# Turning the result column of a decode block: one TensorE transpose and a copy in place of four VectorE transposes

## The chip, the cores and the metric

The kernel runs on one core of a Trainium2 chip. The metric is the device time of one execution in microseconds (us), on the device. The profile's span, from the first to the last instruction, is about 2 us shorter.

## The reference, cut to what matters

One token goes through a pre-norm attention block with a key/value cache of 65,536 positions and then through a gated feed-forward block. What matters here is the last line: the result is 1024 bfloat16 numbers, 2 KB.

```python
h  = x + attention(layernorm(x), k_cache, v_cache, wq, wo)      # 4 kv heads, Sk = 65536, Dh = 128
h2 = h + (gelu(hn @ w_gate) * (hn @ w_up)) @ w_down             # hn = layernorm(h); D = 1024, F = 3584
return h2                                                       # (1, 1, 1024), bfloat16
```

## The kernel before

The last product, with w_down, ends in column form. `dl_ps` is a tile of 128 partitions by 8 columns in PSUM: partition p of column c holds output number 128c + p. In memory, 128 consecutive numbers belong to one c. So the column has to be turned into 8 rows of 128 before the output DMA can write runs of 256 bytes. The kernel before does that with VectorE, in four transposes of 32x32 blocks:

```python
    o_blk = rows.tile([P, 32], BF16, name="o_blk")
    nc.vector.memset(o_blk[:], 0.0)
    o_tr = rows.tile([32, P], BF16, name="o_tr")
    # ... the matmuls of w_down: chunks 0..13 into d_ps, turned early into hd_cp with the residual;
    # ... chunks 14..27 into dl_ps, 8 matmuls of 128x1 for each chunk
    nc.vector.tensor_tensor(out=o_blk[:, 0:DC], in0=dl_ps[:], in1=hd_cp[:], op=ALU.add)
    for i in range(4):
        nc.vector.transpose(out=o_tr[:, 32 * i:32 * i + 32], in_=o_blk[32 * i:32 * i + 32, :])
    nc.sync.dma_start(out=out[0, 0].rearrange("(c p) -> c p", p=P), in_=o_tr[0:DC, :])
```

One more place matters, because it already does what the change will do. After the attention, `oT_all` (128x32, bfloat16) is turned by a TensorE transpose and copied out of PSUM:

```python
    nc.tensor.transpose(out=o_ps[:], in_=oT_all[:], identity=ident_bf[:])     # PSUM tile "oh_ps", 32x128 bf16
    nc.vector.tensor_copy(out=o_sb[:], in_=o_ps[:])
```

Of the kernel before, what the change touches and what calls it, by code (L numbers as in the profile page):

```python
# [9 lines left out]
ALU = mybir.AluOpType  # L10
AX = mybir.AxisListType
BF16 = mybir.dt.bfloat16
# [5 lines left out]
def kernel(  # L18
# [13 lines left out]
    nc = tc.nc  # L32
    P = 128
# [6 lines left out]
    DC = D // P  # L40
# [29 lines left out]
    ident_bf = lead.tile([P, P], BF16, name="ident_bf")  # L70
# [114 lines left out]
    for hf in range(2):  # L185
        for t in range(2):
            o = W2 * hf + rep * t
            nc.vector.tensor_copy(out=qsel[64 * t:64 * t + 64, :, :, hf, o:o + rep],
                                  in_=qsel_ps[64 * t:64 * t + 64, :, :].rearrange("p a (g h) -> p g a h", h=rep))
# [152 lines left out]
    rows = ctx.enter_context(tc.tile_pool(name="rows", bufs=1))  # L342
    ps_w = ctx.enter_context(tc.tile_pool(name="ps_w", bufs=4, space=PSUM))
    ps_t = ctx.enter_context(tc.tile_pool(name="ps_t", bufs=3, space=PSUM))
# [16 lines left out]
    for wc in range(Hq // WN):  # L361
        wv = load(wo_v[:, wc * WN:(wc + 1) * WN, :], "wo_sb")
        for cc in range(WN):
            c = wc * WN + cc
# [14 lines left out]
    def cp_sum(row, add, name):  # L379
        ps = ps_t.tile([P, 4, DS], F32, name=name + "_ps", tag="T")  # L380
        for b in range(4):
            nc.tensor.matmul(ps[:, b, :], lhsT=row[:, b * P:(b + 1) * P], rhs=hsel[:], start=True, stop=True)
        t = rows.tile([P, DC], F32, name=name)
        nc.vector.tensor_tensor(out=t[:].rearrange("p (s b) -> p b s", b=4), in0=ps[:],
                                in1=add[:].rearrange("p (s b) -> p b s", b=4), op=ALU.add)
        return t
# [56 lines left out]
    d_ps = row_bank("d_ps")  # L443
    dl_ps = ps_w.tile([P, DC], F32, name="dl_ps", tag="w")
    nc.vector.memset(dl_ps[:], 0.0)
    o_blk = rows.tile([P, 32], BF16, name="o_blk")
    nc.vector.memset(o_blk[:], 0.0)
    o_tr = rows.tile([32, P], BF16, name="o_tr")
    c0 = 0
    for sz in sizes:  # L450
        wv = load(wd_v[:, c0:c0 + sz, :], "wd_sb")
        for cc in range(sz):
            c = c0 + cc
# [7 lines left out]
        if c0 == NW:  # L461
            d_r = rows.tile([P, 512], F32, name="d_r")
            nc.vector.tensor_copy(out=d_r[:], in_=d_ps[:])
            hd_cp = cp_sum(d_r, h_cp, "hd_cp")
    nc.vector.tensor_tensor(out=o_blk[:, 0:DC], in0=dl_ps[:], in1=hd_cp[:], op=ALU.add)
    for i in range(4):
        nc.vector.transpose(out=o_tr[:, 32 * i:32 * i + 32], in_=o_blk[32 * i:32 * i + 32, :])
    nc.sync.dma_start(out=out[0, 0].rearrange("(c p) -> c p", p=P), in_=o_tr[0:DC, :])


# [28 lines left out]
```

## Time and profile before

| what | value | where read |
|---|---|---|
| time | 412.35 us, three runs from 412.31 to 412.57 | the runs |
| span of the profile | 410.6 us | the page |
| HBM traffic | 173.02 MB, 421 GB/s | the page |
| last TensorE burst ends, last add starts | 407.43, 407.47 us | timeline |
| end of the add to the issue of the output DMA | 0.94 us | timeline |
| issue to end of span | 2.0 us | timeline, span |

These are lines from the page of the kernel before. (PE is TensorE, PEld its weight load, DVE VectorE, ACT ScalarE, SP SyncE; a q at the end means that engine's instruction queue, from which DMAs are issued.) The first line is the busy share of the DMA engines in 40 equal slices of the span, in tenths; then the traffic; then the chain of work that ended last, by engine.

```profile
DMA  8999999999999999999999999999999999999993
...
HBM read 173.02 MB, written 0.00 MB: 421 GB/s over the span
...
DMA 51%; PE 21%; ACT 5%; DVE 4%; issue 1%; DVEq 0%
```

Memory is busy until the last slice, which alone shows 3 instead of 9. That last slice is 10 us long, and it is where the changed lines run. The timeline of the kernel before, for its last microseconds, has start, duration, engine, line, operation, output<-inputs and shapes, and in brackets how long the engine was idle and what released it:

```profile
406.42 1.01 PE L458 MATMUL dl_ps<-act_bf,wd_sb 128*128 128x1 bf16 x24 [0.18 <-DMA wd_sb<-in_B_w_down_dram]
407.47 0.17 DVE L465 TENSOR_TENSOR o_blk<-dl_ps,hd_cp 128x8 bf16<-128x8 f32 x1 [3.37 <-PE dl_ps L458]
407.67 0.84 DVE L467 STREAM_TRANSPOSE o_tr<-o_blk 32x32 bf16<-32x32 bf16 x4
408.58 0.36 SPq L468 DMA_DIRECT2D out_dram<-o_tr  x1
```

The reader is to see a strict sequence: matmuls, add, four transposes, DMA issue. No other engine works any more. The add ends at 407.47 + 0.17 = 407.64; 408.58 - 407.64 = 0.94 us is what the change can alter. The same timeline 65 us earlier shows the turn of `oT_all`, a ready-made price tag for the new sequence:

```profile
342.76 0.17 DVE L307 TENSOR_TENSOR oT_all<-o_ps,rl 128x8 bf16<-128x8 f32 x1 [1.97 <-PE o_ps L305]
...
342.98 0.29 PE L333 MATMUL oh_ps<-ident_bf,oT_all 128*32 128x128 bf16 x1 [0.26 <-DVE oT_all L307]
...
343.31 0.21 DVE L335 COPY o_sb<-oh_ps 32x128 bf16<-32x128 bf16 x1 [0.38 <-PE oh_ps L333]
```

From the end of that add (342.93) to the end of the copy (343.52) it is 0.59 us.

### The profile page before, as it was taken

To read this page: it belongs to the slowest core of one execution; us is meant where nothing else is said; L and a number is where in the kernel's file an instruction comes from. 1 tells how busy PE (TensorE), PEld (TensorE's weight loads), DVE (VectorE), ACT (ScalarE), POOL (GpSimd) and SP (SyncE) were. 2 spreads that over 40 slices of the span, in tenths; PEclk is the share of its full clock that TensorE was granted. 3 is DMA by queue.
4 is the path that set the end of the run, shared out by engine and by line. 5 is a ranking of instruction groups with operands and counts; after the bars stand their busy time and mean duration, and the time that the engine had idled before them with its cause. 6 is when DMAs were issued, how large, how long until landed. Compare 5 with 4: busy or idle time off the path is not lost.

```text
span 410.6 us, 6002 instructions
## 1 busy us (share of the span) xinstructions
PE 272.3 (66%) x2576; PEld 193.8 (47%) x2576; DVE 169.5 (41%) x296; ACT 163.0 (40%) x249; POOL 5.1 (1%) x16
## 2 busy tenths in 40 slices
PE   0448888797993938965868399394945536467365
PEld 0227666484673727645565277182822113163134
DVE  0213787766772636751627187344630001021011
ACT  0014676597570748642524775152738000000000
POOL 1000000000000000000000000000020000000000
PEclk9986999969998887996969689979875655556665
DMA  8999999999999999999999999999999999999993
GB/s 358 409 456 410 450 414 442 425 436 429 434 433 434 433 429 437 421 444 426 437 427 433 431 431 436 429 425 439 428 437 428 441 426 434 428 433 439 421 422 149
DMA packets 6682, 173.40 MB, mean 422 GB/s; under 512 B 896, under 2 KB 896, under 8 KB 1152
## 3 DMA queue, kind: packets, MB, share of 16 engines
q1 hardware_dynamic: 6496, 173.02, 98.0%
q8 instruction: 20, 0.33, 0.3%
q14 instruction: 6, 0.05, 0.0%
q10 hardware_dynamic: 160, 0.00, 0.0%
HBM read 173.02 MB, written 0.00 MB: 421 GB/s over the span
## 4 chain that ended last, share of the span: by engine, by line
DMA 51%; PE 21%; ACT 5%; DVE 4%; issue 1%; DVEq 0%
DMA k_sb<-in_A_k_cache_dram 27%; PE kt_ps L216 13%; DMA wu_sb<-in_B_w_up_dram 10%; DMA v_sb<-in_A_v_cache_dram 10%; DMA wd_sb<-in_B_w_down_dram 5%; ACT pT L272 4%; PE qk_ps L239 3%; PE acc_ps L289 2%; ACT kt_sb L220 2%; DVE mx L246 1%; PE wu_ps L158 1%; DVE kt_sb L222 1%; DVE sc_sb L245 1%; PE o_ps L305 1%; PE bc_ps L262 0%
## 5 line engine op out<-in xcount | busy, mean ns | idle before, releaser
L216 PE MATMUL kt_ps<-ident_f,k_sb 128*128 128x128 f32 x1024 | 144.7, 304 | 37.2 <-DMA k_sb<-in_A_k_cache_dram 34.2
L216 PEld LDWEIGHTS kt_ps<-ident_f,k_sb 128*128 128x128 f32 x1024 | 131.7, 159 | 57.8 <-issue 36.5
L220 ACT COPY kt_sb<-kt_ps 128x1024 bf16<-128x1024 bf16 x116 | 111.9, 1015 | 105.4 <-issue 74.7
L222 DVE COPY kt_sb<-kt_ps 128x1024 bf16<-128x1024 bf16 x140 | 95.3, 688 | 92.8 <-PE kt_ps L216 89.8
L272 ACT ACTIVATE pT<-sc_sb,nbias 128x256 bf16<-128x256 f32 x64 | 47.6, 745 | 23.7 <-DVE nbias L264 23.7
L239 PE MATMUL qk_ps<-kt_sb,qsel 128*32 128x512 bf16 x512 | 39.7, 384 | 9.9 <-ACT kt_sb L220 9.2
L289 PE MATMUL acc_ps<-v_sb,pT 128*32 128x512 bf16 x512 | 37.4, 441 | 12.1 <-DMA v_sb<-in_A_v_cache_dram 12.1
L246 DVE TENSOR_REDUCE mx<-sc_sb 128x8 f32<-128x512 f32 x32 | 35.2, 1099 | 0.5
L245 DVE STREAM_TRANSPOSE sc_sb<-qk_ps 128x512 f32<-128x512 f32 x32 | 23.0, 717 | 19.1 <-PE qk_ps L239 18.8
L289 PEld LDWEIGHTS <-pT 128*32 128x32 bf16 x512 | 17.2, 107 | 28.4 <-issue 19.7
L165 ACT COPY wg_ev<-wg_ps 96x512 f32<-96x512 f32 x1 | 0.6, 582 | 59.3 <-PE wg_ps L158 59.3
L239 PEld LDWEIGHTS <-qsel 128*32 128x32 bf16 x512 | 8.4, 94 | 24.4 <-DVE kt_sb L222 15.2
L298 PE MATMUL l_ps<-lpart,ones_f 128*128 128x8 f32 x16 | 3.8, 312 | 21.7 <-ACT pT L272 21.7
L298 PEld LDWEIGHTS l_ps<-lpart,ones_f 128*128 128x128 f32 x16 | 3.2, 250 | 24.0 <-ACT pT L272 23.1
L158 PEld LDWEIGHTS <-hnz 128*32 128x32 bf16 x112 | 5.2, 131 | 17.6 <-issue 16.0
L158 PE MATMUL wu_ps<-wu_sb,hnz 128*32 128x512 bf16 x56 | 7.2, 625 | 8.8 <-DMA wu_sb<-in_B_w_up_dram 8.8
L353 PE MATMUL at_ps<-wo_sb,o2z 128*32 128x512 bf16 x64 | 7.2, 629 | 8.3 <-DMA wo_sb<-in_A_wo_dram 8.3
L302 DVE COPY acc_sb<-acc_ps 128x512 f32<-128x512 f32 x4 | 2.7, 684 | 22.6 <-PE acc_ps L289 22.6
L272 ACT ACTIVATION_READ_ACCUMULATOR pT<-sc_sb,nbias 128x1 f32 x64 | 12.0, 187 | 0.0
L165 ACT ACT_TABLE_LOAD x1 | 1.3, 1283 | 25.9 <-DVE q_ev L163 25.9
L125 PE MATMUL ln_tot<-ln_s,ones_f 128*128 128x1 f32 x4 | 1.2, 362 | 13.8 <-DVE ln_s L123 13.8
L353 PEld LDWEIGHTS <-o2z 128*32 128x32 bf16 x64 | 2.7, 139 | 12.0 <-issue 11.5
(107 smaller groups left out, 93.5 us busy)
## 6 DMA issues: line engine op xcount, KB each, us to landing
k_sb<-in_A_k_cache_dram SPq DMA_DIRECT2D x16, 4096.0 KB, 40.0
v_sb<-in_A_v_cache_dram SPq DMA_DIRECT2D x16, 4096.0 KB, 37.6
wq_sb<-in_A_wq_dram SPq DMA_DIRECT2D x2, 4096.0 KB, 16.8
wo_sb<-in_A_wo_dram SPq DMA_DIRECT2D x2, 4096.0 KB, 43.1
wg_sb<-in_B_w_gate_dram SPq DMA_DIRECT2D x2, 3584.0 KB, 43.5
wu_sb<-in_B_w_up_dram SPq DMA_DIRECT2D x2, 3584.0 KB, 40.6
wd_sb<-in_B_w_down_dram SPq DMA_DIRECT2D x1, 3584.0 KB
wd_sb<-in_B_w_down_dram SPq DMA_DIRECT2D x1, 1792.0 KB, 29.7
```

Of the source, the lines that this page charges most:

```text
L158: nc.tensor.matmul(banks[s // 4][32 * g:32 * g + 32, :], lhsT=stat, rhs=mov(s), start=first, stop=last, tile_position=(0, 32 * g))
L216: nc.tensor.transpose(out=kt_ps[:, b, :], in_=k32s[m0 // 16][:, m0 % 16, :], identity=ident_f[:])
L220: nc.scalar.copy(out=dst_bf, in_=src_bf)
L222: nc.vector.tensor_copy(out=dst_bf, in_=src_bf)
L239: nc.tensor.matmul(qk_ps[32 * c:32 * c + 32, :], lhsT=qsel[:, g, par, hf, :], rhs=mv[:, :, 32 * c:32 * c + 32, par], start=(hf == 0 and pa ...
L245: nc.vector.transpose(out=sl.rearrange("p n h -> p (n h)"), in_=qk_ps[:])
L246: nc.vector.tensor_reduce(out=st["mx"][:, :, pi], in_=sl.rearrange("p n h -> p h n"), axis=AX.X, op=ALU.max)
L272: nc.scalar.activation(out=pT[:, :, r, :], in_=sc_sb[:, hf * HG * TG:(hf + 1) * HG * TG, r].rearrange("p (a t) -> p a t", t=TG), func=ACT. ...
L289: nc.tensor.matmul(acc[32 * c:32 * c + rep * TG, :], lhsT=pTs[a // HG][:, a % HG, :, :].rearrange("p r t -> p (r t)"), rhs=v_sb[:, i * TG: ...
L298: nc.tensor.matmul(l_ps[:], lhsT=ones_f[:], rhs=lpart[:, hf, :], start=(hf == 0), stop=(hf == NH - 1))
L305: nc.tensor.matmul(o_ps[:], lhsT=acc_sb[:, t * Dh:(t + 1) * Dh], rhs=sel[:, t:rep * TG:TG], start=(t == 0), stop=(t == TG - 1))
L353: nc.tensor.matmul(bank[32 * g:32 * g + 32, :], lhsT=stat, rhs=w2[:, s * 512:(s + 1) * 512], start=first, stop=last, tile_position=(0, 32 ...
```

## The change

The intent: round the result to bfloat16 in the add, turn the 128x8 column by one TensorE transpose into 8x128 in PSUM, and copy it out once, instead of four VectorE instructions one after the other. The padded tile and its memset go away.

```diff
-    o_blk = rows.tile([P, 32], BF16, name="o_blk")
-    nc.vector.memset(o_blk[:], 0.0)
-    o_tr = rows.tile([32, P], BF16, name="o_tr")
+    o_col = rows.tile([P, DC], BF16, name="o_col")
 ...
-    nc.vector.tensor_tensor(out=o_blk[:, 0:DC], in0=dl_ps[:], in1=hd_cp[:], op=ALU.add)
-    for i in range(4):
-        nc.vector.transpose(out=o_tr[:, 32 * i:32 * i + 32], in_=o_blk[32 * i:32 * i + 32, :])
-    nc.sync.dma_start(out=out[0, 0].rearrange("(c p) -> c p", p=P), in_=o_tr[0:DC, :])
+    nc.vector.tensor_tensor(out=o_col[:], in0=dl_ps[:], in1=hd_cp[:], op=ALU.add)
+    oT_ps = ps_t.tile([DC, P], BF16, name="oT_ps", tag="T")
+    nc.tensor.transpose(out=oT_ps[:], in_=o_col[:], identity=ident_bf[:])
+    o_row = rows.tile([DC, P], BF16, name="o_row")
+    nc.vector.tensor_copy(out=o_row[:], in_=oT_ps[:])
+    nc.sync.dma_start(out=out[0, 0].rearrange("(c p) -> c p", p=P), in_=o_row[:])
```

## The prediction

> **What bounds the kernel now.** Reading memory. The page puts HBM traffic at 173.0 MB, 421 GB/s over the span of 410.6 us, and the DMA row of the 40 slices stands at 9 from the second slice to the last but one. The chain that ended last gives 51% to DMA, 21% to PE, 4% to DVE. The changed lines run once, after the last weight slice has landed (about 406.4 us in the timeline), when nothing else is left to do, so every nanosecond of them is on the chain.
>
> **The tail before (timeline, last 13 us).** The last TensorE burst into dl_ps ends at 407.43. The add (o_blk) starts at 407.47, takes 0.167 us and ends at 407.64. The four 32x32 VectorE transposes start at 407.67, take 200 ns each and 0.84 us together, and end at 408.51. The output DMA is issued at 408.58. From the end of the add to the issue: 0.94 us. From the issue to the end of the span: 2.0 us.
>
> **What the change removes.** The four transposes with their gaps (0.87 us after the add), and a 72 ns memset at 299.6 us, which I count as nothing.
>
> **What it adds.** One TensorE transpose with its weight load and one VectorE copy of 8x128 bf16 out of PSUM, with two hand-overs between engines. The kernel already does almost this sequence at 342.8 us: oT_all (128x32, bf16) is turned by a bf16 transpose with the same identity moving, and copied out. There the add ended at 342.93, weight load and transpose started at 342.98 (transpose 288 ns), the copy started at 343.31 and took 211 ns, ending at 343.52: 0.59 us from the end of the add to the end of the copy. The granted clock is 0.50 in both places (windows view), so the durations carry over. The copy's cost should follow its 128 elements in a row, not its partitions (8 instead of 32). The Trainium skill, "TensorE: Matmul & The Clock Gate", Part 4, gives 275 to 390 ns for a 128x128 bf16 transpose; the 288 ns here agree. "VectorE: DVE Perf Modes", rules for kernel authors, calls the VectorE path fastest for a 32x32 block; here there are four in a row, 0.84 us, which makes the TensorE path competitive.
>
> **Sum.** Add to issue: before 0.94 us, after 0.59 + 0.07 = 0.66 us. Gain about 0.28 us, all of it on the chain; the output DMA has the same shape (8 partitions of 128 bf16, 2 KB). 412.35 - 0.28 = 412.07, so I predict 412.1 us: 0.07% faster, as large as the spread of the three runs of before (0.26 us). The range 411.6 to 412.6 should hold it 8 times in 10; its width is shifts between builds in the memory-bound part, not doubt about the tail. Chances: faster by over 2% 0.005, within 2% 0.99, slower by over 2% 0.005.
>
> **What would show it right.** In the timeline after: the weight load of o_col about 0.05 us after the add, a transpose of about 0.29 us, a copy of about 0.21 us starting 0.33 us after the transpose's start, and the DMA issue 0.66 us after the add. From issue to end still 2.0 us. The stages before 406 us unchanged to a few tenths.
>
> **What would make it wrong.** A copy of 8 partitions slower than that of 32; a TensorE hand-over that costs more right after the burst of 128x1 matmuls than at 342.9 us; an instruction fetch falling into the tail; or a shift of a few tenths in when the big loads start, which would hide or outweigh 0.28 us. A change of over 2% (8 us) has no place to come from.

## The result

| kernel | median of 6 runs | lowest to highest |
|---|---|---|
| before | 412.42 us | 412.22 to 412.57 |
| after | 412.09 us | 412.00 to 412.40 |

The ratio of after to before is 0.9994, with a 95% interval from 0.9981 to 1.0007. (A ratio here is the mean time of one kernel's fast runs over that of the other's of the same rounds, so it is not quite the ratio of the medians.) In the total time the two kernels are therefore the same: the medians differ by 0.33 us, and the interval contains 1. The prediction was 412.1 us.

This is the timeline of the kernel after, in the lines that answer to those of before:

```profile
406.32 1.01 PE L456 MATMUL dl_ps<-act_bf,wd_sb 128*128 128x1 bf16 x24 [0.21 <-DMA wd_sb<-in_B_w_down_dram]
407.37 0.17 DVE L463 TENSOR_TENSOR o_col<-dl_ps,hd_cp 128x8 bf16<-128x8 f32 x1 [3.41 <-PE dl_ps L456]
407.58 0.08 PEld L465 LDWEIGHTS <-o_col 128*8 128x8 bf16 x1 [0.34 <-DVE o_col L463]
407.59 0.27 PE L465 MATMUL oT_ps<-ident_bf,o_col 128*8 128x128 bf16 x1 [0.26 <-DVE o_col L463]
407.89 0.21 DVE L467 COPY o_row<-oT_ps 8x128 bf16<-8x128 bf16 x1 [0.36 <-PE oT_ps L465]
408.18 0.36 SPq L468 DMA_DIRECT2D out_dram<-o_row  x1
```

The add ends at 407.54 and the issue comes at 408.18: 0.64 us instead of 0.94. The transpose took 266 ns (288 predicted), the copy 211 ns (as at 343 us, though it has 8 partitions instead of 32). From the issue to the end of the span (410.2) it is 2.0 us, as before. The two spans differ by 0.4 us: 0.30 from the turn, and 0.10 because the last burst began 0.10 us earlier. That start lies before the turn and moves from trace to trace: in all the traces of this case but rows4 the last add starts between 407.16 and 407.57 us, in no order that follows the kind of turn.

The page of after shows that the rest is as it was:

```profile
HBM read 173.02 MB, written 0.00 MB: 422 GB/s over the span
...
DMA 51%; PE 21%; ACT 6%; DVE 4%; issue 2%; DVEq 0%
```

### The profile page after: what moved, and what is told of

It reads as the page before. It is cut to its first block, busy times and chain, and to the rows that moved or that the text cites. A ratio compares the mean times of both kernels' runs of the same rounds, so it can differ in the third digit from the quotient of the medians.

```text
span 410.2 us, 5998 instructions
## 1 busy us (share of the span) xinstructions
PE 271.7 (66%) x2577; PEld 193.1 (47%) x2577; DVE 168.9 (41%) x292; ACT 162.9 (40%) x249; POOL 5.1 (1%) x16
## 4 chain that ended last, share of the span: by engine, by line
DMA 51%; PE 21%; ACT 6%; DVE 4%; issue 2%; DVEq 0%
DMA k_sb<-in_A_k_cache_dram 27%; PE kt_ps L216 13%; DMA wo_sb<-in_A_wo_dram 11%; DMA wu_sb<-in_B_w_up_dram 10%; ACT pT L272 4%; DMA wd_sb<-in_B_w_down_dram 3%; PE qk_ps L239 3%; ACT kt_sb L220 2%; PE acc_ps L289 2%; DVE mx L246 1%; PE at_ps L353 1%; PE wu_ps L158 1%; DVE kt_sb L222 1%; DVE sc_sb L245 1%; PE o_ps L305 1%
```

## The experiments

A difference of 0.3 us in 412 is as large as what separates single runs, so the total time alone proves little. The theories to tell apart were:

- TAIL: the turn got 0.30 us shorter, nothing else is going on at that time, and all of it reaches the total time.
- SHIFT: the difference comes from tenths of a microsecond in the memory-bound part (0.10 us of it is in the pair of traces above).
- MEMSET: the memset that was taken away moved VectorE's order in the attention, and that is the gain.
- COUNT: TensorE has no part in it; the old turn was slow only because VectorE ran four instructions where one would do.

All runs below gave the right result except where "wrong" is said. Times are medians, and "before" is the kernel before in the rounds of the same call. The calls ran on different chips, so each kernel is set against the before of its own call.

| kernel | us | before, us | add to issue | issue to end of span |
|---|---|---|---|---|
| aa | 412.60 | 412.45 | 0.95 | 2.0 |
| after_again | 412.12 | 412.45 | 0.65 | 2.0 |
| after_memset | 412.12 | 412.45 | 0.64 | 2.0 |
| no_turn (wrong) | 411.71 | 412.45 | 0.07 | 2.2 |
| before_x9 | 421.06 | 412.41 | nine passes | 2.0 |
| after_x9 | 417.33 | 412.41 | nine passes | 2.0 |
| act_copy | 411.99 | 412.41 | 0.64 | 2.0 |
| one_dve | 412.46 | 412.41 | 0.27 (first of four) | 2.9 |
| after_x9s | 418.29 | 412.52 | nine passes | 2.0 |
| one_dve_1dma (wrong) | 412.05 | 412.52 | 0.31 | 2.2 |
| direct | 425.51 | 412.52 | 0.07 | 15.5 |
| rows4 | 414.51 | 412.52 | 0.08 (after the copy) | 2.5 |

### aa: how small a difference can be seen

No edit: the kernel before against itself.

> The kernel before, unchanged, against itself: it measures how far two builds of one program differ here. All theories: ratio 1.000, median within 0.2 us of before. The width of its interval says whether 0.3 us (0.0007 of the time) can be seen at all in the total time. If it differs from before by 0.3 us or more, the total time can't carry the verdict and only the trace of the tail can.

Measured: 412.60 against 412.45 us, ratio 1.0003, interval 0.9991 to 1.0016. One program against itself differed by 0.15 us, and the interval is 1.0 us wide (0.0025 of 412). The total time of single kernels can't carry a verdict about 0.3 us.

### after_again and after_memset: the same gain, with and without the memset

`after_again` is the changed kernel. `after_memset` puts the padded tile back:

```diff
-    o_col = rows.tile([P, DC], BF16, name="o_col")
+    o_blk = rows.tile([P, 32], BF16, name="o_blk")
+    nc.vector.memset(o_blk[:], 0.0)
 ...
-    nc.tensor.transpose(out=oT_ps[:], in_=o_col[:], identity=ident_bf[:])
+    nc.tensor.transpose(out=oT_ps[:], in_=o_blk[:, 0:DC], identity=ident_bf[:])
```

> The changed kernel once more, in five rounds. Theory TAIL (the turn between the last add and the output DMA got 0.30 us shorter, 0.94 to 0.64 us, and nothing hides it): 0.3 us faster than before, ratio 0.9993; in the trace add-to-issue 0.64 us again. Theory SHIFT (the difference comes from when the big loads run, not from the turn): a difference that changes its size or sign against the first comparison, while the last weight slice lands at a different time.

> The changed kernel's turn, but with the 128x32 tile and its 72 ns memset put back: only the turn itself differs from before. TAIL: the memset costs nothing, 0.3 us faster than before, as after_again. Theory MEMSET (the removed memset moved VectorE's work in the attention and that gives the gain): same time as before, about 412.4 us.

Measured: 412.12 us for both, against 412.45; ratios 0.9997 (0.9985 to 1.0010; two of its five runs took 412.64 and 412.92, so in the means only 0.1 us is left) and 0.9993 (0.9980 to 1.0007). MEMSET falls: with the memset back, the gain of 0.33 us in the medians stays, and so does the short turn in the trace. In the medians the difference kept its sign and its size three times (0.33 us each), but no interval here excludes SHIFT. The traces say more. First after_again, then after_memset, the add and the DMA issue:

```profile
407.40 0.17 DVE L463 TENSOR_TENSOR o_col<-dl_ps,hd_cp 128x8 bf16<-128x8 f32 x1 [2.98 <-PE dl_ps L456]
...
408.22 0.36 SPq L468 DMA_DIRECT2D out_dram<-o_row  x1
```

```profile
407.27 0.17 DVE L464 TENSOR_TENSOR o_blk<-dl_ps,hd_cp 128x8 bf16<-128x8 f32 x1 [3.30 <-PE dl_ps L457]
...
408.08 0.37 SPq L469 DMA_DIRECT2D out_dram<-o_row  x1
```

Counted from the start of the last add to the end of the span, whatever came earlier drops out. The spans in the traces are, to two decimals, 410.62 (before), 410.71 (aa), 410.21 (after), 410.25 (after_again) and 410.11 (after_memset). So this stretch is 3.15 us in before and in aa, and 2.84, 2.85 and 2.84 us in the three kernels with the new turn. The 0.3 us are in the tail, and SHIFT accounts only for the scatter around it.

### no_turn: the whole turn taken away (wrong)

```diff
-    oT_ps = ps_t.tile([DC, P], BF16, name="oT_ps", tag="T")
-    ... transpose, o_row, copy
-    nc.sync.dma_start(out=out[0, 0].rearrange("(c p) -> c p", p=P), in_=o_row[:])
+    nc.sync.dma_start(out=out[0, 0].rearrange("(p c) -> p c", c=DC), in_=o_col[:])
```

> Wrong on purpose: the result column is written out as 128 runs of 16 bytes, in the wrong order, with no transpose and no copy. It takes the whole turn away. TAIL: add-to-issue falls from 0.64 to about 0.11 us (one hand-over), so 0.53 us less than the changed kernel and 0.83 us less than before, about 411.6 us, ratio 0.998, if the output DMA takes its 2.0 us from issue to end as before. SHIFT: no clear difference from the changed kernel. If 128 short runs cost more than 8 runs of 256 bytes, the stretch from issue to end grows above 2.0 us and shows by how much.

The timeline of no_turn:

```profile
407.57 0.17 DVE L463 TENSOR_TENSOR o_col<-dl_ps,hd_cp 128x8 bf16<-128x8 f32 x1 [3.90 <-PE dl_ps L456]
407.81 0.35 SPq L464 DMA_DIRECT2D out_dram<-o_col  x1
```

Add to issue is 0.07 us (407.81 - 407.74), so the changed turn costs 0.64 - 0.07 = 0.57 us. But the 128 runs of 16 bytes need longer: the span ends at 410.05, 2.24 us after the issue instead of the 2.03 of the changed kernel (410.21 - 408.18). (An expectation below has 2.29 and 2.02, from spans rounded to 0.1 us.) By the trace the sum is 0.57 - 0.21 = 0.36 us less than the changed kernel; the medians show 412.12 - 411.71 = 0.41. Against before the ratio is 0.9985, interval 0.9972 to 0.9997: this is clear of 1. Taking the turn away is seen in the total time, as TAIL says, although the 0.53 us that I had expected against the changed kernel did not all arrive.

### before_x9, after_x9, after_x9s: the turn nine times

To lift the cost out of the noise, add and turn were repeated nine times on the same data:

```diff
+    for rep_i in range(9):
         nc.vector.tensor_tensor(...)   # the last add
         # before_x9: the four VectorE transposes; after_x9: TensorE transpose and copy
```

> The last add and the four VectorE transposes nine times in a row instead of once (same result). One pass takes 1.07 us in the trace of before, from the start of the add to the end of the last transpose with a gap. TAIL: 8 more passes add 8 x 1.07 = 8.5 us, all of it to the time: about 420.9 us. SHIFT or anything that hides the tail: clearly less than that.

> The last add, the TensorE transpose and the copy nine times in a row. One pass takes 0.76 us in the trace of after. TAIL: 8 more passes add 6.1 us to the changed kernel, about 418.2 us, and it is 2.4 + 0.3 = 2.7 us faster than before_x9, nine times the 0.30 us of one pass. If the hand-overs between engines cost more when repeated, or less because weights load early, the difference is not nine times 0.30.

`before_x9` took 421.06 us, 8.65 more than before. The timeline of its first passes:

```profile
407.34 0.17 DVE L466 TENSOR_TENSOR o_blk<-dl_ps,hd_cp 128x8 bf16<-128x8 f32 x1 [2.95 <-PE dl_ps L458]
407.54 0.84 DVE L468 STREAM_TRANSPOSE o_tr<-o_blk 32x32 bf16<-32x32 bf16 x4
408.42 0.17 DVE L466 TENSOR_TENSOR o_blk<-dl_ps,hd_cp 128x8 bf16<-128x8 f32 x1
```

The last of the nine adds starts at 415.94, so a pass takes (415.94 - 407.34) / 8 = 1.075 us, and 8 of them 8.60 us: the whole of it reaches the total time. That part of TAIL is settled.

`after_x9` took 417.33 us, though, not 418.2. Its timeline:

```profile
407.34 0.17 DVE L466 TENSOR_TENSOR o_col<-dl_ps,hd_cp 128x8 bf16<-128x8 f32 x1 [3.92 <-PE dl_ps L456]
...
407.56 0.27 PE L467 MATMUL oT_ps<-ident_bf,o_col 128*8 128x128 bf16 x1 [0.26 <-DVE o_col L466]
407.86 0.21 DVE L468 COPY o_row<-oT_ps 8x128 bf16<-8x128 bf16 x1 [0.36 <-PE oT_ps L467]
408.00 0.14 DVE L466 TENSOR_TENSOR o_col<-dl_ps,hd_cp 128x8 bf16<-128x8 f32 x1
```

The next add starts at 408.00, before the copy's record ends (407.86 + 0.21 = 408.07). It writes another tile and needn't wait for the copy to be complete. The DMA of the real kernel must wait. So a pass here is only 0.645 us, and the comparison was not fair to the old turn, whose adds start after the last transpose has ended. The experiment was mended: in `after_x9s` add and copy write overlapping parts of one tile.

```diff
-    o_col = rows.tile([P, DC], BF16, name="o_col")
-    o_row = rows.tile([DC, P], BF16, name="o_row")
+    o_both = rows.tile([P, P], BF16, name="o_both")
+    o_col, o_row = o_both[:, 0:DC], o_both[0:DC, :]
```

> The changed kernel's add, TensorE transpose and copy nine times, as after_x9, but add and copy write overlapping parts of one tile, so that each add has to wait for the copy before it to be complete. In after_x9 the next add started 0.14 us after the copy's start, though the copy takes 0.21, so a pass was 0.645 us; in before_x9 every add waited for the last transpose. If that overlap is the whole reason why the two nine-fold kernels were 3.7 us apart and not 2.7, a pass takes 0.76 us now (0.17 + 0.05 + 0.30 + 0.21 + 0.03), the kernel 412.1 + 8 x 0.76 = 418.2 us, 2.8 us less than before_x9's 421.06. If it still takes 417.3 us, the turn itself got cheaper than I read from one pass.

It took 418.29 us. The timeline of its first passes:

```profile
407.24 0.17 DVE L466 TENSOR_TENSOR o_both<-dl_ps,hd_cp 128x8 bf16<-128x8 f32 x1 [2.87 <-PE dl_ps L457]
...
407.77 0.21 DVE L468 COPY o_both<-oT_ps 8x128 bf16<-8x128 bf16 x1 [0.36 <-PE oT_ps L467]
408.01 0.17 DVE L466 TENSOR_TENSOR o_both<-dl_ps,hd_cp 128x8 bf16<-128x8 f32 x1
```

Now the add waits until 408.01 for a copy that ends at 407.98, and a pass is 0.77 us. The difference of one pass, 1.075 - 0.77 = 0.30 us, is the same as in the single turn. The two kernels ran in different calls, so each is set against its own before: 8.65 us over it against 5.77 us over it, which is 2.88 us apart, or 0.32 us for each of nine turns. The two intervals, 1.0193 to 1.0223 and 1.0126 to 1.0154, lie well apart. This shows that the TensorE turn is 0.3 us shorter than the four VectorE transposes and that this time lies on the path to the end.

### act_copy: the copy on ScalarE

```diff
-    nc.vector.tensor_copy(out=o_row[:], in_=oT_ps[:])
-    nc.sync.dma_start(...)
+    nc.scalar.copy(out=o_row[:], in_=oT_ps[:])
+    nc.scalar.dma_start(...)
```

> The changed kernel with the copy out of PSUM on ScalarE instead of VectorE, and the output DMA issued by ScalarE's own queue. TAIL: the time follows this one copy and the hand-over after it. If ScalarE's copy of 8x128 takes 0.2 us as VectorE's does and the hand-over to the issuing queue stays 0.07 us or shrinks, the same time as the changed kernel within 0.05 us; ScalarE is slower per instruction elsewhere in this trace (1015 against 688 ns for 128x1024), so up to 0.15 us slower is possible.

The timeline of act_copy:

```profile
407.73 0.26 ACT L467 COPY o_row<-oT_ps 8x128 bf16<-8x128 bf16 x1 [13.64 <-PE oT_ps L465]
408.01 0.31 ACTq L468 DMA_DIRECT2D out_dram<-o_row  x1
```

The copy is 0.05 us slower (0.26 against 0.21), and the hand-over to its own queue shorter (0.02 us instead of 0.08). Add to issue is 0.64 us again, and the time is 411.99 against 412.41 us, ratio 0.9988 (0.9973 to 1.0003). It makes no difference that could be shown.

### one_dve and one_dve_1dma: one VectorE transpose for all four blocks

One instruction over 128 partitions transposes the four blocks in place. Then the result lies in four groups of 8 partitions, and four DMAs write it, two from each of two queues:

```diff
+    nc.vector.transpose(out=o_tr[:], in_=o_blk[:])            # o_tr is 128x32
+    o_v = out[0, 0].rearrange("(c i q) -> i c q", i=4, q=32)
+    for i in range(4):
+        eng = nc.sync if i % 2 == 0 else nc.scalar
+        eng.dma_start(out=o_v[i], in_=o_tr[32 * i:32 * i + DC, :])
```

> The rival to the changed turn: VectorE transposes all four 32x32 blocks in one instruction over 128 partitions (about 0.20 us as each of the four now), and four output DMAs of 8 runs of 64 bytes follow, two issued by SyncE and two by ScalarE. Theory COUNT (the old turn was slow only because VectorE ran four instructions one after the other; the gain doesn't need TensorE): the first issue comes 0.30 us after the add instead of 0.94. But the second issue of each queue starts 0.36 us later, at 0.66 us, so the end comes as with the changed kernel, about 412.1 us, within 0.1 us.

The timeline of one_dve:

```profile
407.16 0.17 DVE L465 TENSOR_TENSOR o_blk<-dl_ps,hd_cp 128x8 bf16<-128x8 f32 x1 [3.70 <-PE dl_ps L458]
407.36 0.21 DVE L466 STREAM_TRANSPOSE o_tr<-o_blk 128x32 bf16<-128x32 bf16 x1
407.60 0.65 ACTq L470 DMA_DIRECT2D out_dram<-o_tr  x2
407.65 0.72 SPq L470 DMA_DIRECT2D out_dram<-o_tr  x2
```

COUNT is half right. One instruction does in 0.21 us what four did in 0.84, and the first issue comes 0.27 us after the add (407.60 - 407.33). Yet the time is 412.46 us, no better than before: my expectation of 412.1 was a miss. From the first issue to the end of the span it takes 2.9 us (410.5 - 407.60).

`one_dve_1dma` keeps the single transpose and writes with one DMA of 32 runs of 64 bytes. Its values are wrong:

```diff
-    (the four DMAs)
+    nc.sync.dma_start(out=out[0, 0].rearrange("(k q) -> k q", q=32), in_=o_tr[0:32, :])
```

> Wrong on purpose: as one_dve, but after the single VectorE transpose only one output DMA, of 32 runs of 64 bytes from 32 partitions (right number of bytes, wrong values). It tells apart why one_dve gained nothing. If the four DMAs ate the gain: add-to-issue 0.30 us and from issue to end about 2.0 us, about 411.8 us, 0.3 us less than the changed kernel. If 64-byte runs out of a VectorE transpose are slow by themselves: from issue to end 2.3 us or more, as long as with four DMAs less the 0.36 us of the second issue, and 412.1 us or more.

The timeline of one_dve_1dma:

```profile
407.35 0.17 DVE L465 TENSOR_TENSOR o_blk<-dl_ps,hd_cp 128x8 bf16<-128x8 f32 x1 [2.91 <-PE dl_ps L458]
407.55 0.21 DVE L466 STREAM_TRANSPOSE o_tr<-o_blk 128x32 bf16<-128x32 bf16 x1
407.83 0.36 SPq L467 DMA_DIRECT2D out_dram<-o_tr  x1
```

It took 412.05 us against 412.52, ratio 0.9987 (0.9974 to 0.9999), with 0.31 us from add to issue and 2.2 us to the end (410.0 - 407.83). So the gain of one_dve went into the way its four DMAs write: 2.9 - 2.2 = 0.7 us more after the first issue. (The single DMA also reads other partitions and uses one queue instead of two, so the number of DMAs is not the only difference.) About 0.4 of that is the wait of each queue for its second issue; the other 0.3 us was not traced further. The 32 runs of 64 bytes cost 0.15 us more than the 8 runs of 256 bytes of before (2.19 - 2.04, with the unrounded spans). The result lies between the two branches of the expectation: my 411.8 was too low by 0.25 us, of which 0.15 is this cost; the rest is within what single builds differ by.

What the TensorE turn buys is therefore not the fastest transpose. It is a layout that one DMA writes; a right single DMA from the layout of the one VectorE transpose was not tried.

### direct: no transpose, 1024 runs of 2 bytes

```diff
-    (transpose, copy, DMA from o_row)
+    nc.sync.dma_start(out=out[0, 0].rearrange("(c p) -> c p", p=P), in_=o_col[:])
```

> Right result with no transpose at all: the output DMA reads the column and writes 1024 runs of 2 bytes. It shows why the column is turned. no_turn's 128 runs took 2.29 us from issue to end against 2.02 of 8 runs, 0.27 us for 120 runs more; in proportion 1024 runs add 2.3 us, so about 4.3 us from issue to end and about 413.8 us. TAIL needs only that add-to-issue stays 0.07 us, as in no_turn.

Right result, 425.51 us. The DMA issues of direct, in the DMA view of its tail (median us from issue to landing at the end of the line):

```profile
out_dram<-o_col SPq DMA_DIRECT2D x1, 2.0 KB, 14.6
```

The same view of no_turn shows what 128 runs of 16 bytes take:

```profile
out_dram<-o_col SPq DMA_DIRECT2D x1, 2.0 KB, 1.4
```

The scaling in proportion to the number of runs was far off: I expected 4.3 us from issue to end and it is 15.5. The Trainium skill, "DMA: Bandwidth & Descriptors", table of specifications, says that transfers below 512 B make the DMA engine read, modify and write; runs of 16, 64 and 256 bytes are all below that and still landed in 1.4 us or ended within 2.3 us, so the threshold alone doesn't explain the 2-byte case. The trace narrows it down. These are the packet counts of direct's DMA view, first from 408 to 410 us, then from 409.5 to 423:

```profile
DMA packets 1040, 0.00 MB, mean 1 GB/s; under 512 B 1040, under 2 KB 1040, under 8 KB 1040
...
DMA packets 0, 0.00 MB, mean 0 GB/s; under 512 B 0, under 2 KB 0, under 8 KB 0
```

All packets are over by 409.5, 2 us after the issue, but the DMA lands at 407.54 + 14.6 = 422.1. The long time lies between the last packet on record and the landing. What happens in it stays open. The run does show why turning the column pays at all: 0.57 us of turn save 13 us of DMA.

### rows4: a version that needs no turn

An attempt to beat both. The residual and all 28 chunks are summed as four rows of 256 in one PSUM bank, so that after the last chunk only a copy and the DMA are left.

```diff
+    for g in range(4):      # x and the attention output go into the bank early
+        nc.tensor.matmul(r_ps[32*g:32*g+32, 0:256], lhsT=ident_bf[0:4, g:g+32], rhs=x_row[:], start=True, ...)
+        nc.tensor.matmul(r_ps[32*g:32*g+1, 0:256], lhsT=hsel[:, g//2:g//2+1], rhs=at_r[:, 256*(g%2):256*(g%2)+256], ...)
 ...
+            for g in range(4):      # for each chunk c
+                nc.tensor.matmul(r_ps[32*g:32*g+32, 0:256], lhsT=actz[:, c, :], rhs=wv[:, cc, 256*g:256*g+256], ...)
-    (d_ps, dl_ps, hd_cp, add, transposes)
+    nc.vector.tensor_copy(out=o_row[:], in_=r_ps[:, 0:256])
+    nc.sync.dma_start(out=out[0, 0].rearrange("(g n) -> g n", n=256), in_=o_row[0::32, :])
```

> A version made to beat both: nothing is turned at the end. The residual row and all 28 chunks of the last product are summed in one PSUM bank as four rows of 256 (x and the attention output put in early by small matmuls, each chunk by four 128x32 stationaries side by side), and after the last chunk one VectorE copy of 128x256 to bfloat16 and an output DMA of 4 runs of 512 bytes are left. TAIL: last burst 0.65 to 0.9 us instead of 1.01, copy 0.40 us (between 0.17 for 8 and 0.69 for 512 columns), hand-overs 0.04 and 0.07, then 2.0 us: 0.5 us less than the changed kernel, about 411.6 us. If the four side-by-side matmuls are held up by their weight loads, the burst is 1.2 us or more and half of that gain is gone.

It took 414.51 us, ratio 1.0047 (1.0033 to 1.0060): 0.5% slower, and a miss by 2.9 us. The timeline of rows4:

```profile
408.15 1.06 PE L441 MATMUL r_ps<-wd_sb,actz 128*32 128x256 bf16 x12 [0.22 <-DMA wd_sb<-in_B_w_down_dram]
...
409.26 0.42 DVE L445 CAST o_row<-r_ps 128x256 bf16<-128x256 f32 x1 [11.68 <-PE r_ps L441]
409.76 0.66 SPq L446 DMA_DIRECT2D out_dram<-o_row  x1
```

Two things went wrong. First, the last burst starts at 408.15 instead of the 406.42 of before. Most of that lateness is there long before the tail. Two of the long waits for memory in the chain that ended last (start, duration), for before:

```profile
99.01 31.64 DMA k_sb<-in_A_k_cache_dram
...
297.06 39.35 DMA v_sb<-in_A_v_cache_dram
```

and for rows4:

```profile
100.57 30.45 DMA k_sb<-in_A_k_cache_dram
...
299.71 38.27 DMA v_sb<-in_A_v_cache_dram
```

The wait for keys starts 1.56 us later, but it ends only 0.37 us later (131.02 against 130.65): most of that delay is absorbed. The wait for values ends 1.57 us later (337.98 against 336.41), and from there on the lateness stays, at 1.6 to 1.8 us. So it builds up in the memory-bound part between 131 and 338 us. A lower granted clock is not enough to explain it: from 287 to 297 us rows4 has 0.66 where before has 0.86, but act_copy has 0.71 there and its wait for values ends at 336.28, no later than that of before. The rewrite also changed the order of instructions in the attention stage; what brought the lateness was not tested. Second, even the tail by itself is not better than that of the changed kernel: from the start of the last burst to the end of the span it is 4.10 us (412.25 - 408.15), against 3.89 (410.21 - 406.32). The burst took 1.06 us instead of the 0.65 to 0.9 expected, and the DMA issue 0.66 us instead of 0.36, with 2.5 us from issue to end instead of 2.0. The copy took 0.42 us, as estimated. The version is dropped.

## Why the prediction was right

The prediction was 412.1 us in a range of 411.6 to 412.6; measured were 412.09 and 412.12. That the total came within 0.01 us is luck: one program against itself differed by 0.15 us, and a gain of zero or of 0.6 us would have fallen into the range as well. What was tested is the account of the tail, in the traces and with the nine-fold kernels. Point by point:

1. The changed lines run once, "so every nanosecond of them is on the chain". Shown: eight more passes of the old turn, 8 x 1.075 = 8.60 us in the trace, cost 8.65 us of total time.
2. "0.59 us from the end of the add to the end of the copy", taken from the turn of `oT_all`. It was 0.56 us (407.54 to 408.10), because the transpose took 266 ns instead of 288. The granted clock is 0.50 in both places, as stated. The Trainium skill's 275 to 390 ns for a 128x128 transpose ("TensorE: Matmul & The Clock Gate", Part 4) holds the 288 ns and lies just above the 266; the turns here have 32 and 8 columns instead of 128.
3. "The copy's cost should follow its 128 elements in a row, not its partitions." Shown for the partitions: 211 ns for 8 and for 32. The length of the row was not varied.
4. "Add to issue: before 0.94 us, after 0.59 + 0.07 = 0.66 us. Gain about 0.28 us". It was 0.64 us and 0.30; the nine-fold kernels give 0.30 in the trace and 0.32 in the time for each turn.
5. The memset "which I count as nothing". after_memset agrees: 412.12 us with it as without it, though 72 ns could not be seen in these totals.
6. The range's "width is shifts between builds in the memory-bound part, not doubt about the tail". Confirmed in kind: 0.10 us of the 0.4 us between the spans came from an earlier burst, and the kernel before differed from itself by 0.15 us.
7. "Here there are four in a row, 0.84 us, which makes the TensorE path competitive." Right for what was compared, but too narrow: one VectorE instruction could have transposed all four blocks in 0.21 us. The Trainium skill's rule that VectorE is fastest for 32x32 blocks ("VectorE: DVE Perf Modes", rules for kernel authors) agrees with that. What stands against it is the layout: four DMAs ate the gain.

The same mechanism explains why so little came of it. The turn was 0.94 us out of 412, so nothing done to it could be worth more than about 0.2%.

## What to carry to other kernels

Price a new sequence of instructions from a place in the same trace where the kernel already does it, hand-overs included; that gave 0.59 us where 0.56 was measured. When the difference is below the noise, repeat the piece, and make sure that the repetition keeps the wait that the real kernel has, or it measures throughput instead of latency. For a small result at the very end, the number of output DMAs and the length of their runs weigh as much as the transpose.

## What the Trainium skill lacked or had wrong

- "DMA: Bandwidth & Descriptors" warns of transfers below 512 B and gives overheads for each packet, but no time for a store to memory in very short runs. Here one DMA of 2 KB landed after 1.4 us in 128 runs of 16 bytes, and after 14.6 us in 1024 runs of 2 bytes, 12.6 us or more of it after the last packet on record.
- The same page fits a fixed cost of about 2.0 us for one DMA, on the path issued by GpSimd (Anatomy of one DMA), and has no such fit for the path issued by SyncE. For the SyncE queue here, issue to landing of 2 KB was 1.4 us (no_turn, one_dve_1dma); issue to the end of the whole program was 2.0 us for 8 runs of 256 bytes.
- "VectorE: DVE Perf Modes", the three transpose paths, gives times for 128x128 only. The runs show 200 ns for one 32x32 bfloat16 block and 210 ns for four blocks in one instruction over 128 partitions. The page says that the blocks are transposed independently; what that costs when rows have to be written is not there: four DMAs took 0.7 us more here than the one of one_dve_1dma, whose values are wrong.
- "VectorE: DVE Perf Modes", The DRAIN you can't avoid, reports that waiting on a semaphore after each of eight copies cost nothing extra. Between a small copy and a small add here it did: 0.77 us for a pass that waits for the copy against 0.645 us for one that doesn't. The section's other sentence, that an instruction which is not held starts earlier, agrees: the add started 0.14 us after the start of a copy that took 0.21.
